# Ten 16 KB load slots become five of 32 KB, and the activation rows move to every eighth column

## The chip, the cores and the metric

The kernel runs on one core of a Trainium2 chip. The metric is the device time of one execution in microseconds (us), the median of several runs of the same program. Five engines of the core work side by side: TensorE (PE in the profile; its weight loads are PEld), VectorE (DVE), ScalarE (ACT), GpSimd (POOL) and SyncE (SP). Sixteen DMA engines carry data between device memory (DRAM) and the on-chip memory of 128 partitions. A DMA is issued by an engine's queue: SP issues all loads of weights and caches, ACT issues the load of `x`, and both issue the result. A DMA is cut into packets, here one for each contiguous run of a partition. In the trace a transfer of weights has 128 packets and sixteen landings, one for each engine's share; the instructions that read its data start after the last of the sixteen.

## What is computed

One decoding step of a transformer block for a batch of 4, one token each, in bf16:

```python
h  = x + attention(layernorm(x)) @ wo        # x: 4 x 1 x 1024
h2 = h + (silu(n @ w1) * (n @ w3)) @ w2      # n = layernorm(h)

# attention: 32 query heads of 128, 4 key/value heads, the last 2048 cached positions
q = layernorm(x) @ wq                        # wq: 1024 x 4096
p = softmax(q @ k.T * 128**-0.5)             # k, v: 4 x 4 x 2048 x 128 of the cache
o = p @ v                                    # wo: 4096 x 1024
# w1, w3: 1024 x 3584, w2: 3584 x 1024
```

The inputs that must be read are 55.57 MB: the two caches' windows, `wq` and `wo` 8.39 MB each (33.55 MB together), `w1`, `w3` and `w2` 7.34 MB each. Every byte is used once, with four rows of activations, so the arithmetic is small beside the reading.

## The kernel before

**The ring of loads.** The list `ring` names every load in its order: the keys of the four batch rows (`k`), the four parts of `wq` with four places `kT` for the transposed keys between them, the values `v`, `wo`, `w1`, `w3` and `w2`. `fill()` (line 118 of the profile issues the DMA) takes the next item while fewer than ten are open, gives it a slot of 8192 bf16 columns (16 KB on each partition, `NSLOT = 10`, `SLOT = 8192`), and issues its DMA from SP. `done(name, i)` marks an item as read and calls `fill()` again. A DMA waits on SP until the slot that it is given is free; as SP's queue is in order, all later loads wait behind it. A place `kT` has no DMA, but takes a slot. So there are 20 MB of slots, and the loads run some way ahead of the work.

The transfers are: `k`, `wq`, `v`, `wo` four each, of 2 MB in packets of 16 KB; `w1` and `w3` four each, of 1.75 MB in packets of 14 KB (two rows of 3584 columns a partition); `w2` five, of 8, 8, 8, 2 and 2 rows of 1024 columns (16 KB and 4 KB a partition). That is 29.

**The order of the work** is the order of the program text (the schedule is manual):

- `x` is loaded in four DMAs from ACT (line 134), a quarter of its columns each, to the partitions 32c to 32c+3. `layernorm_T` works on its transpose, where the batch is 4 of 32 columns.
- Keys: 256 transposes on PE (line 226), copied out of PSUM by DVE and ACT (lines 228, 230).
- `q`: for each part of `wq`, matmuls of 32 columns of activations against 512 columns of the weights, four of them side by side in the array (line 244). The four parts have 16 matmuls each.
- For each batch row scores (line 279), row maximum, softmax on ACT (line 319), transpose of the probabilities on DVE (line 331), output (line 354); the rows are staggered, so that the output of row b follows the scores of row b+3.
- `wo` (line 419), the sum with `x`, the second `layernorm_T`.
- `up_projection` for `w1`, then for `w3` (line 443), with silu on ACT and DVE in between (lines 457 to 461); the product `hg` (line 465) and its transpose `hg_T` (line 210, a helper).
- `w2` (line 476), the last sum `res` (line 486), and the result in four DMAs of four rows of 256 columns, two on SP and two on ACT (line 489).

Of the kernel before, what the change touches and what calls it, by code (L numbers as in the profile page):

```python
# [10 lines left out]
P = 128  # L11
ACT = mybir.ActivationFunctionType
ALU = mybir.AluOpType
AX = mybir.AxisListType
BF16 = mybir.dt.bfloat16
FP32 = mybir.dt.float32

NSLOT = 10
SLOT = 8192
NEG = -1.0e30  # L20


# [1 line left out]
def kernel(  # L24
# [20 lines left out]
    nc = tc.nc  # L45

    B, _, D = A_x.shape
    Hkv, Sk, Dh = A_k_cache.shape[1], A_k_cache.shape[2], A_k_cache.shape[3]
    NQ = A_wq.shape[1]
# [6 lines left out]
    NK = W // P  # L56
    C = 4
    R = 32
    DQ = D // C
    FQ = F // C  # L60
    FH = FQ // 2
# [8 lines left out]
    T = REP  # L70
# [18 lines left out]
    def of_cache(cache, b):  # L89
        return cache[b, :, Sk - W : Sk, :].rearrange("g (i j) d -> i g (j d)", j=JR)  # L90

    ks = [("k", b, [JR, Dh], of_cache(A_k_cache, b)) for b in range(B)]
    vs = [("v", b, [JR, Dh], of_cache(A_v_cache, b)) for b in range(B)]
    kts = [("kT", b, [JR, P], None) for b in range(B)]
    wqs = [("wq", i, [2, NQ], wq_v[:, 2 * i : 2 * i + 2, :]) for i in range(KC // 2)]
    wos = [("wo", g, [1, T * D], wo_v[:, g : g + 1, :]) for g in range(Hkv)]
    ring = ks + [x for two in zip(kts, wqs) for x in two] + vs + wos
    for name, w_v in (("w1", w1_v), ("w3", w3_v)):
        for i in range(KC // 2):
            ring.append((name, i, [2, F], w_v[:, 2 * i : 2 * i + 2, :]))  # L100
    W2B = [8, 8, 8, 2, 2]
    f0 = 0
    for i, n in enumerate(W2B):
        ring.append(("w2", i, [n, D], w2_v[:, f0 : f0 + n, :]))
        f0 += n
    place = {(name, i): at for at, (name, i, _, _) in enumerate(ring)}
    views = []
    used = set()

    def fill():  # L110

        while len(views) < len(ring) and (len(views) < NSLOT or len(views) - NSLOT in used):
            name, i, shape, src = ring[len(views)]
            slot = stream.tile([P, SLOT], BF16, tag="slot", name="s_" + name)
            dst = slot[:, : int(np.prod(shape))]
            view = dst.rearrange("p (a b) -> p a b", a=shape[0])
            if src is not None:
                nc.sync.dma_start(out=dst if name in ("k", "v") else view, in_=src)  # L118
            views.append(view)

    def get(name, i):
        return views[place[(name, i)]]

    def done(name, i):
        used.add(place[(name, i)])
        fill()

    ctx.enter_context(tc.manual_schedule())
# [1 line left out]

    x_nat = act.tile([P, DQ], BF16)
    nc.vector.memset(x_nat[:], 0.0)
    for c in range(C):
        nc.scalar.dma_start(out=x_nat[R * c : R * c + B, :], in_=x_flat[:, c * DQ : (c + 1) * DQ])
    fill()

    ident = const.tile([P, P], BF16)
# [39 lines left out]
    def layernorm_T(h_T, tag):  # L177

        both = act.tile([P, 2, KC, B], FP32, tag=tag + "_both")
        nc.vector.tensor_copy(out=both[:, 0], in_=h_T[:, :, :B])  # L180
        nc.vector.tensor_tensor(out=both[:, 1], in0=both[:, 0], in1=both[:, 0], op=ALU.mult)  # L181
        sums_ps = ps.tile([P, 2, KC, B], FP32, tag="kt3")
        nc.tensor.matmul(sums_ps[:], lhsT=ones_f[:], rhs=both[:], start=True, stop=True)  # L183
        sums = act.tile([P, 2, B], FP32, tag=tag + "_sums")
        nc.vector.tensor_reduce(
            out=sums[:], in_=sums_ps[:].rearrange("p t k b -> p t b k"), axis=AX.X, op=ALU.add
        )
        mean = act.tile([P, 2, B], FP32, tag=tag + "_mean")
        nc.vector.tensor_single_scalar(out=mean[:], in_=sums[:], scalar=1.0 / D, op=ALU.mult)
        rstd = act.tile([P, 1, B], FP32, tag=tag + "_rstd")  # L190
        nc.vector.tensor_tensor(out=rstd[:, 0], in0=mean[:, 0], in1=mean[:, 0], op=ALU.mult)
        nc.vector.tensor_tensor(out=rstd[:, 0], in0=mean[:, 1], in1=rstd[:, 0], op=ALU.subtract)  # L192
        nc.scalar.activation(  # L193
            out=rstd[:, 0], in_=rstd[:, 0], func=ACT.Sqrt, bias=eps_t[:], scale=1.0
        )
        nc.vector.reciprocal(out=rstd[:, 0], in_=rstd[:, 0])
        n_T = act.tile([P, KC, R], BF16, tag=tag + "_nT")
        nc.gpsimd.memset(n_T[:], 0.0)
        hc = act.tile([P, KC, B], FP32, tag=tag + "_hc")
        nc.vector.tensor_tensor(  # L200
            out=hc[:], in0=both[:, 0], in1=mean[:, 0:1, :].to_broadcast([P, KC, B]), op=ALU.subtract
        )
        nc.vector.tensor_tensor(
            out=n_T[:, :, :B], in0=hc[:], in1=rstd[:].to_broadcast([P, KC, B]), op=ALU.mult
        )
        return n_T

# [26 lines left out]

    q_ps = [ps.tile([P, REP // 2, Dh], FP32, tag=f"sc{hf}", name=f"q_ps{hf}") for hf in range(2)]
    HALF = REP // 2
    for i in range(KC // 2):
        w = get("wq", i)
        for kk in range(2):
            kc = 2 * i + kk  # L240
            for hf in range(2):
                for c in range(C):
                    o = (2 * c + hf) * HALF * Dh
                    nc.tensor.matmul(  # L244
                        q_ps[hf][R * c : R * c + R],
                        lhsT=xn_T[:, kc, :],
                        rhs=w[:, kk, o : o + HALF * Dh],
                        start=(kc == 0),
                        stop=(kc == KC - 1),
                        tile_position=(0, R * c),  # L250
                    )
        done("wq", i)
# [10 lines left out]
    for b in range(B):  # L263
        nc.vector.tensor_copy(  # L264
            out=Qm[:, b].rearrange("p (g y) -> p g y", y=QW)[:, :, :REP],
            in_=qT_ps[:, :, :, b].rearrange("p r g -> p g r"),
        )


# [122 lines left out]
    for l in range(2):  # L392
# [12 lines left out]
    oP = act.tile([P, Hkv, T, R], BF16)  # L405
    nc.gpsimd.memset(oP[:], 0.0)
    nc.vector.tensor_copy(
        out=oP[:, :, :, :B],
        in_=oX[:, :, : Hkv * B].rearrange("p t (g b) -> p g t b", b=B),
    )  # L410

# [21 lines left out]


    def up_projection(name, out_ps):
        for i in range(KC // 2):
            w = get(name, i)
            for kk in range(2):
                kc = 2 * i + kk
                for hf in range(2):  # L440
                    for c in range(C):
                        o = c * FQ + hf * FH
                        nc.tensor.matmul(  # L443
                            out_ps[hf][R * c : R * c + R],
                            lhsT=hn_T[:, kc, :],
                            rhs=w[:, kk, o : o + FH],
                            start=(kc == 0),
                            stop=(kc == KC - 1),
                            tile_position=(0, R * c),
                        )  # L450
            done(name, i)
# [32 lines left out]
            fc += 1  # L484
    res = act.tile([P, DQ], BF16)
    nc.vector.tensor_tensor(out=res[:], in0=y2_ps[:], in1=h1[:], op=ALU.add)  # L486
    for c in range(C):
        eng = nc.sync if c % 2 == 0 else nc.scalar
        eng.dma_start(out=out_flat[:, c * DQ : (c + 1) * DQ], in_=res[R * c : R * c + B, :])


# [28 lines left out]
```

## Time and profile before

| | before |
|---|---|
| median of three runs | 140.28 us (140.24 to 140.34) |
| the profiled execution | 140.35 us, of which the span shown is 138.5 us |
| packets of the SP and ACT queues' DMA, share of 16 engines | 94.8% of the span |
| read from DRAM | 55.58 MB, 401 GB/s over the span |
| PE busy, granted clock | 76.9 us (55%), 0.787 |
| DVE, ACT busy | 52.5 us, 43.2 us |
| transfers of weights and caches | 29 |

The span runs from the first to the last instruction. The 1.85 us between it and the profiled execution's time lie around it. The row of packets says how much of the sixteen DMA engines' time was taken by data. Busy times of the engines are sums over stages with different limits, so they are read beside the chain of work that ended last, which the profile follows back from the last instruction. For a transfer, the time from issue to landing holds its wait behind earlier transfers of the queue.

### The profile page before, as it was taken

How to read it: one execution, taken by the hardware profiler on the slowest of the kernel's cores; microseconds unless marked ns; L12 is line 12 of the kernel's file. 1: busy time of each engine (PE TensorE's matmuls, PEld its weight loads, DVE VectorE, ACT ScalarE, POOL GpSimd, SP SyncE). 2: the span in 40 equal slices, each digit the busy share in tenths (PEclk: the TensorE clock that was granted, in tenths of full speed). 3: DMA queues.
4: the chain of work that ended last, by engine and by line, in shares of the span. 5: the costliest groups of instructions: out<-in, count | busy, mean ns of one | idle time of the engine just before them, and what ended most of it. 6: DMA issues, size and time to landing. Idle time of an engine off the chain costs nothing.

```text
span 138.5 us, 2042 instructions
## 1 busy us (share of the span) xinstructions
PE 76.9 (55%) x868; PEld 45.8 (33%) x868; DVE 52.5 (38%) x97; ACT 43.2 (31%) x57; POOL 4.2 (3%) x18
## 2 busy tenths in 40 slices
PE   0009999971153799059639979483632432352280
PEld 0009988851011332024223535372311110142150
DVE  3026566630000334457365595515249700610001
ACT  2103799970000508999419600000420000000000
POOL 7400000000000000000000000000000000000000
PEclk9999999999555559955995999999999555555555
DMA  4999999999999999999999999999999999999940
GB/s 147 403 432 445 426 416 440 421 421 435 426 421 440 421 428 426 416 435 435 416 435 433 416 440 410 435 414 435 418 431 426 426 427 431 421 435 431 390 182 2
DMA packets 4249, 55.72 MB, mean 402 GB/s; under 512 B 496, under 2 KB 528, under 8 KB 784
## 3 DMA queue, kind: packets, MB, share of 16 engines
q1 hardware_dynamic: 4192, 55.58, 94.8%
q8 instruction: 7, 0.11, 0.3%
q10 hardware_dynamic: 48, 0.01, 0.0%
q14 instruction: 2, 0.02, 0.0%
HBM read 55.58 MB, written 0.01 MB: 401 GB/s over the span
## 4 chain that ended last, share of the span: by engine, by line
DMA 68%; PE 18%; DVE 6%; ACT 4%; issue 1%; SPq 1%; DVEq 0%
DMA s_w<-in_B_w_dram 38%; DMA s_wq<-in_A_wq_dram 24%; PE o_ps L354 10%; DMA s_k<-in_A_k_cache_dram 6%; ACT P L319 4%; PE sc_ps L279 4%; DVE PT L331 2%; PE q_ps L244 1%; PE nm_ps L308 1%; SPq L118 1%; DVE rmax L293 1%; PE mx_ps L295 1%; PE qT_ps L258 1%; DVE om L371 1%; PE tot_ps L340 1%
## 5 line engine op out<-in xcount | busy, mean ns | idle before, releaser
L319 ACT ACTIVATE P<-sc_ps,bias 128x512 bf16<-128x512 f32 x16 | 19.7, 1420 | 9.9 <-DVE bias L316 9.9
L226 PE MATMUL kt_ps<-ident,s_k 128*128 128x128 bf16 x256 | 18.4, 232 | 0.3
L226 PEld LDWEIGHTS <-s_k 128*128 128x128 bf16 x256 | 16.8, 105 | 1.9 <-issue 1.2
L354 PE MATMUL o_ps<-s_v,PT 128*128 128x512 bf16 x64 | 17.5, 435 | 0.0
L230 ACT COPY s_kT<-kt_ps 128x1024 bf16<-128x1024 bf16 x16 | 16.2, 1012 | 2.2 <-PE kt_ps L226 1.3
L443 PE MATMUL gu_ps<-s_w,n_T 128*32 128x448 bf16 x128 | 9.2, 435 | 13.4 <-DMA s_w<-in_B_w_dram 11.6
L228 DVE COPY s_kT<-kt_ps 128x1024 bf16<-128x1024 bf16 x16 | 11.1, 691 | 6.0 <-PE kt_ps L226 6.0
L476 PE MATMUL y_ps<-s_w,hg_T 128*32 128x256 bf16 x112 | 6.7, 416 | 9.4 <-DMA s_w<-in_B_w_dram 9.4
L244 PE MATMUL q_ps<-s_wq,n_T 128*32 128x512 bf16 x64 | 5.9, 503 | 10.4 <-DMA s_wq<-in_A_wq_dram 10.4
L331 DVE STREAM_TRANSPOSE PT<-P 128x2048 bf16<-128x2048 bf16 x4 | 9.2, 2302 | 2.7 <-ACT P L319 2.7
L354 PEld LDWEIGHTS <-PT 128*128 128x128 bf16 x64 | 7.1, 116 | 8.9 <-issue 4.2
L443 PEld LDWEIGHTS <-n_T 128*32 128x32 bf16 x128 | 3.9, 109 | 18.0 <-issue 14.6
L279 PE MATMUL sc_ps<-s_kT,Qm 128*32 128x512 bf16 x64 | 8.8, 608 | 0.4 <-DVE Qm L264 0.4
L193 ACT ACTIVATE rstd<-rstd,eps_t 128x4 f32<-128x4 f32 x2 | 0.6, 298 | 26.7 <-DVE rstd L192 26.7
L476 PEld LDWEIGHTS <-hg_T 128*32 128x32 bf16 x112 | 4.7, 138 | 11.7 <-issue 7.6
L183 PE MATMUL sums_ps<-both,ones_f 128*128 128x64 f32 x4 | 1.1, 374 | 11.9 <-DVE both L181 11.9
L254 DVE CAST q_sb<-q_ps 128x512 bf16<-128x512 f32 x1 | 0.7, 692 | 15.5 <-PE q_ps L244 15.5
L244 PEld LDWEIGHTS <-n_T 128*32 128x32 bf16 x64 | 2.0, 112 | 13.4 <-issue 12.7
L363 DVE SCALAR_TENSOR_TENSOR od<-o_ps,rinv,jmask 128x512 f32<-128x512 f32 x4 | 3.0, 750 | 8.0 <-PE o_ps L354 7.9
L295 PE MATMUL mx_ps<-ident_f,rmax 128*1 128x128 f32 x8 | 1.9, 333 | 7.4 <-DVE rmax L293 7.4
L459 DVE RECIPROCAL eg<-eg 128x896 f32<-128x896 f32 x1 | 5.8, 5754 | 0.0
L486 DVE TENSOR_TENSOR res<-y_ps,h 128x256 bf16<-128x256 f32 x1 | 0.4, 425 | 13.6 <-PE y_ps L476 13.6
(68 smaller groups left out, 62.4 us busy)
## 6 DMA issues: line engine op xcount, KB each, us to landing
s_w<-in_B_w_dram SPq DMA_DIRECT2D x8, 1792.0 KB, 25.4
s_k<-in_A_k_cache_dram SPq DMA_DIRECT2D x4, 2048.0 KB, 14.0
s_wq<-in_A_wq_dram SPq DMA_DIRECT2D x4, 2048.0 KB, 20.5
s_v<-in_A_v_cache_dram SPq DMA_DIRECT2D x4, 2048.0 KB, 27.9
s_wo<-in_A_wo_dram SPq DMA_DIRECT2D x4, 2048.0 KB, 27.4
s_w<-in_B_w_dram SPq DMA_DIRECT2D x3, 2048.0 KB, 32.7
s_w<-in_B_w_dram SPq DMA_DIRECT2D x2, 512.0 KB, 31.6
x_nat<-in_A_x_dram ACTq DMA_DIRECT2D x4, 2.0 KB
```

The lines of the kernel that those rows point to most:

```text
L226: nc.tensor.transpose(out=kt_ps[:, jj], in_=k[:, jb * JB + jj, :], identity=ident[:])
L228: nc.vector.tensor_copy(out=kT[:, jb * JB : (jb + 1) * JB], in_=kt_ps[:])
L230: nc.scalar.copy(out=kT[:, jb * JB : (jb + 1) * JB], in_=kt_ps[:])
L244: nc.tensor.matmul(q_ps[hf][R * c : R * c + R], lhsT=xn_T[:, kc, :], rhs=w[:, kk, o : o + HALF * Dh], start=(kc == 0), stop=(kc == KC - 1) ...
L279: nc.tensor.matmul(sc_ps[b][R * q : R * q + R], lhsT=Qm[:, b, g * R : (g + 1) * R], rhs=v[:, g, q], start=(g == 0), stop=(g == Hkv - 1), t ...
L295: nc.tensor.matmul(mx_ps[:1, :], lhsT=rmax[:], rhs=ident_f[:], start=True, stop=True)
L319: nc.scalar.activation(out=P4[:, :, :, g], in_=sc_ps[b][:].rearrange("p (j i) -> p j i", i=L5), func=ACT.Exp, bias=bias[:, g : g + 1], sca ...
L331: nc.vector.transpose(out=PT[:].rearrange("p j h -> p (j h)"), in_=stage.pop(("P4", b))[:].rearrange("p j i g -> p (j i g)"),)
L354: nc.tensor.matmul(o_ps[:], lhsT=PT[:, i * JM : (i + 1) * JM, :].rearrange("p j h -> p (j h)"), rhs=v[:, i * JM : (i + 1) * JM, :], start= ...
L443: nc.tensor.matmul(out_ps[hf][R * c : R * c + R], lhsT=hn_T[:, kc, :], rhs=w[:, kk, o : o + FH], start=(kc == 0), stop=(kc == KC - 1), til ...
L459: nc.vector.reciprocal(out=eg[:], in_=eg[:])
L476: nc.tensor.matmul(y2_ps[R * c : R * c + R, :], lhsT=hg_T[:, fc, :], rhs=w[:, ff, c * DQ : (c + 1) * DQ], start=(fc == 0), stop=(fc == FC ...
```

## The change

Five slots of 16384 columns (32 KB on each partition) take the place of ten of 8192, so the slots hold the same 20 MB. An entry of the ring is now a list of parts that share a slot: two of `k`, of `kT`, of `v` or of `wo`, each still with a DMA of its own of 2 MB; or one transfer of twice the rows: `wq` in two transfers of four rows (32 KB packets), `w1` and `w3` in two each (28 KB packets), `w2` in 16, 8, 2 and 2 rows, of which the last three share a slot. A slot is free when all of its parts have been read. The loops over `wq`, `w1` and `w3` run over two parts with four rows each, in place of four with two; the matmuls are the same in the same order.

`x` comes in one DMA of 16 rows of 256 columns, to every eighth partition (batch row b of column quarter c at partition 32c+8b, not 32c+b), so that in the transposed forms the batch lies at every eighth of 32 columns; the copies that read or write those columns use a stride of 8. The result goes out in two DMAs of eight rows, one on SP and one on ACT.

```diff
--- before.py
+++ after.py
@@ -15,8 +15,8 @@
 BF16 = mybir.dt.bfloat16
 FP32 = mybir.dt.float32
 
-NSLOT = 10
-SLOT = 8192
+NSLOT = 5
+SLOT = 16384
 NEG = -1.0e30
 
 
@@ -56,6 +56,7 @@
     NK = W // P
     C = 4
     R = 32
+    S = R // B
     DQ = D // C
     FQ = F // C
     FH = FQ // 2
@@ -89,40 +90,55 @@
     def of_cache(cache, b):
         return cache[b, :, Sk - W : Sk, :].rearrange("g (i j) d -> i g (j d)", j=JR)
 
-    ks = [("k", b, [JR, Dh], of_cache(A_k_cache, b)) for b in range(B)]
-    vs = [("v", b, [JR, Dh], of_cache(A_v_cache, b)) for b in range(B)]
-    kts = [("kT", b, [JR, P], None) for b in range(B)]
-    wqs = [("wq", i, [2, NQ], wq_v[:, 2 * i : 2 * i + 2, :]) for i in range(KC // 2)]
-    wos = [("wo", g, [1, T * D], wo_v[:, g : g + 1, :]) for g in range(Hkv)]
-    ring = ks + [x for two in zip(kts, wqs) for x in two] + vs + wos
-    for name, w_v in (("w1", w1_v), ("w3", w3_v)):
-        for i in range(KC // 2):
-            ring.append((name, i, [2, F], w_v[:, 2 * i : 2 * i + 2, :]))
-    W2B = [8, 8, 8, 2, 2]
+    def pair(parts):
+        return [parts[0:2], parts[2:4]]
+
+    k_, v_ = (
+        pair([(name, b, [JR, Dh], of_cache(cache, b)) for b in range(B)])
+        for name, cache in (("k", A_k_cache), ("v", A_v_cache))
+    )
+    kT_ = pair([("kT", b, [JR, P], None) for b in range(B)])
+    wo_ = pair([("wo", g, [1, T * D], wo_v[:, g : g + 1, :]) for g in range(Hkv)])
+
+    def four_rows(name, view, n):
+        return [[(name, i, [4, n], view[:, 4 * i : 4 * i + 4, :])] for i in range(KC // 4)]
+
+    wq_ = four_rows("wq", wq_v, NQ)
+    ring = k_ + wq_[:1] + kT_ + wq_[1:] + v_ + wo_ + four_rows("w1", w1_v, F) + four_rows("w3", w3_v, F)
+    W2B = [16, 8, 2, 2]
+    w2_ = []
     f0 = 0
     for i, n in enumerate(W2B):
-        ring.append(("w2", i, [n, D], w2_v[:, f0 : f0 + n, :]))
+        w2_.append(("w2", i, [n, D], w2_v[:, f0 : f0 + n, :]))
         f0 += n
-    place = {(name, i): at for at, (name, i, _, _) in enumerate(ring)}
-    views = []
+    ring += [w2_[:1], w2_[1:]]
+    views = {}
+    taken = []
     used = set()
 
     def fill():
 
-        while len(views) < len(ring) and (len(views) < NSLOT or len(views) - NSLOT in used):
-            name, i, shape, src = ring[len(views)]
-            slot = stream.tile([P, SLOT], BF16, tag="slot", name="s_" + name)
-            dst = slot[:, : int(np.prod(shape))]
-            view = dst.rearrange("p (a b) -> p a b", a=shape[0])
-            if src is not None:
-                nc.sync.dma_start(out=dst if name in ("k", "v") else view, in_=src)
-            views.append(view)
+        while len(taken) < len(ring):
+            n = len(taken) - NSLOT
+            if n >= 0 and not all((name, i) in used for name, i, _, _ in ring[n]):
+                break
+            parts = ring[len(taken)]
+            slot = stream.tile([P, SLOT], BF16, tag="slot", name="s_" + parts[0][0])
+            o = 0
+            for name, i, shape, src in parts:
+                dst = slot[:, o : o + int(np.prod(shape))]
+                o += int(np.prod(shape))
+                view = dst.rearrange("p (a b) -> p a b", a=shape[0])
+                if src is not None:
+                    nc.sync.dma_start(out=dst if name in ("k", "v") else view, in_=src)
+                views[(name, i)] = view
+            taken.append(slot)
 
     def get(name, i):
-        return views[place[(name, i)]]
+        return views[(name, i)]
 
     def done(name, i):
-        used.add(place[(name, i)])
+        used.add((name, i))
         fill()
 
     ctx.enter_context(tc.manual_schedule())
@@ -130,8 +146,7 @@
 
     x_nat = act.tile([P, DQ], BF16)
     nc.vector.memset(x_nat[:], 0.0)
-    for c in range(C):
-        nc.scalar.dma_start(out=x_nat[R * c : R * c + B, :], in_=x_flat[:, c * DQ : (c + 1) * DQ])
+    nc.scalar.dma_start(out=x_nat[::S, :], in_=x_flat.rearrange("b (c n) -> c b n", c=C))
     fill()
 
     ident = const.tile([P, P], BF16)
@@ -177,7 +192,7 @@
     def layernorm_T(h_T, tag):
 
         both = act.tile([P, 2, KC, B], FP32, tag=tag + "_both")
-        nc.vector.tensor_copy(out=both[:, 0], in_=h_T[:, :, :B])
+        nc.vector.tensor_copy(out=both[:, 0], in_=h_T[:, :, ::S])
         nc.vector.tensor_tensor(out=both[:, 1], in0=both[:, 0], in1=both[:, 0], op=ALU.mult)
         sums_ps = ps.tile([P, 2, KC, B], FP32, tag="kt3")
         nc.tensor.matmul(sums_ps[:], lhsT=ones_f[:], rhs=both[:], start=True, stop=True)
@@ -201,7 +216,7 @@
             out=hc[:], in0=both[:, 0], in1=mean[:, 0:1, :].to_broadcast([P, KC, B]), op=ALU.subtract
         )
         nc.vector.tensor_tensor(
-            out=n_T[:, :, :B], in0=hc[:], in1=rstd[:].to_broadcast([P, KC, B]), op=ALU.mult
+            out=n_T[:, :, ::S], in0=hc[:], in1=rstd[:].to_broadcast([P, KC, B]), op=ALU.mult
         )
         return n_T
 
@@ -234,10 +249,10 @@
 
     q_ps = [ps.tile([P, REP // 2, Dh], FP32, tag=f"sc{hf}", name=f"q_ps{hf}") for hf in range(2)]
     HALF = REP // 2
-    for i in range(KC // 2):
+    for i in range(KC // 4):
         w = get("wq", i)
-        for kk in range(2):
-            kc = 2 * i + kk
+        for kk in range(4):
+            kc = 4 * i + kk
             for hf in range(2):
                 for c in range(C):
                     o = (2 * c + hf) * HALF * Dh
@@ -263,7 +278,7 @@
     for b in range(B):
         nc.vector.tensor_copy(
             out=Qm[:, b].rearrange("p (g y) -> p g y", y=QW)[:, :, :REP],
-            in_=qT_ps[:, :, :, b].rearrange("p r g -> p g r"),
+            in_=qT_ps[:, :, :, S * b].rearrange("p r g -> p g r"),
         )
 
 
@@ -405,7 +420,7 @@
     oP = act.tile([P, Hkv, T, R], BF16)
     nc.gpsimd.memset(oP[:], 0.0)
     nc.vector.tensor_copy(
-        out=oP[:, :, :, :B],
+        out=oP[:, :, :, ::S],
         in_=oX[:, :, : Hkv * B].rearrange("p t (g b) -> p g t b", b=B),
     )
 
@@ -433,10 +448,10 @@
 
 
     def up_projection(name, out_ps):
-        for i in range(KC // 2):
+        for i in range(KC // 4):
             w = get(name, i)
-            for kk in range(2):
-                kc = 2 * i + kk
+            for kk in range(4):
+                kc = 4 * i + kk
                 for hf in range(2):
                     for c in range(C):
                         o = c * FQ + hf * FH
@@ -484,9 +499,9 @@
             fc += 1
     res = act.tile([P, DQ], BF16)
     nc.vector.tensor_tensor(out=res[:], in0=y2_ps[:], in1=h1[:], op=ALU.add)
-    for c in range(C):
-        eng = nc.sync if c % 2 == 0 else nc.scalar
-        eng.dma_start(out=out_flat[:, c * DQ : (c + 1) * DQ], in_=res[R * c : R * c + B, :])
+    out_v = out_flat.rearrange("b (c n) -> c b n", c=C)
+    nc.sync.dma_start(out=out_v[: C // 2], in_=res[: P // 2 : S, :])
+    nc.scalar.dma_start(out=out_v[C // 2 :], in_=res[P // 2 :: S, :])
 
 
 # ---- launch: one core; inputs and outputs as the reference has them ----
```

## The prediction, made before the changed kernel was run

> **What bounds the kernel now.** I read the page's slices first, then the chain that ended last, then the order of time around the places where PE waits for data, and last the waits of the queues.
>
> ```profile
> DMA  4999999999999999999999999999999999999940
> GB/s 147 403 432 445 426 416 440 421 421 435 426 421 440 421 428 426 416 435 435 416 435 433 416 440 410 435 414 435 418 431 426 426 427 431 421 435 431 390 182 2
> ...
> DMA 68%; PE 18%; DVE 6%; ACT 4%; issue 1%; SPq 1%; DVEq 0%
> ```
>
> The DMA engines are full from the second slice to the 38th, at 403 to 445 GB/s, with no hole at any stage. The chain names PE for 18% (the attention), yet the DMA row shows no gap there: the chain follows a wait for a free slot back into PE, while the queue still held work. So the end is set by when the last byte of `w2` lands, plus a tail. Evidence in order of time:
>
> ```profile
> 38.85 1.90 PE L244 MATMUL q_ps<-s_wq,n_T 128*32 128x512 bf16 x16 [3.85 <-DMA s_wq<-in_A_wq_dram]
> 43.75 1.90 PE L244 MATMUL q_ps<-s_wq,n_T 128*32 128x512 bf16 x16 [3.01 <-DMA s_wq<-in_A_wq_dram]
> ...
> 108.76 1.68 PE L443 MATMUL gu_ps<-s_w,n_T 128*32 128x448 bf16 x16 [3.36 <-DMA s_w<-in_B_w_dram]
> 113.06 1.69 PE L443 MATMUL gu_ps<-s_w,n_T 128*32 128x448 bf16 x16 [2.62 <-DMA s_w<-in_B_w_dram]
> ...
> 122.33 1.90 PE L476 MATMUL y_ps<-s_w,hg_T 128*32 128x256 bf16 x32 [3.22 <-DMA s_w<-in_B_w_dram]
> 127.22 1.90 PE L476 MATMUL y_ps<-s_w,hg_T 128*32 128x256 bf16 x32 [3.00 <-DMA s_w<-in_B_w_dram]
> 132.12 2.33 PE L476 MATMUL y_ps<-s_w,hg_T 128*32 128x256 bf16 x40 [3.00 <-DMA s_w<-in_B_w_dram]
> 134.61 0.62 PE L476 MATMUL y_ps<-s_w,hg_T 128*32 128x256 bf16 x8 [0.17 <-DMA s_w<-in_B_w_dram]
> 135.28 0.42 DVE L486 TENSOR_TENSOR res<-y_ps,h 128x256 bf16<-128x256 f32 x1 [13.61 <-PE y_ps L476]
> 135.73 0.66 SPq L489 DMA_DIRECT2D out_dram<-res  x2
> ```
>
> Wherever PE waits for DMA, its starts are one transfer apart: 4.90 us for 2 MB (38.85 to 43.75, 122.33 to 127.22), 4.30 us for 1.75 MB (108.76 to 113.06). Each stage is done 3 us before the next transfer lands. After the last landing come 0.66 us of matmuls, 0.45 us of `res`, then the result's DMAs and the end: 2.8 us from 135.73 to 138.5.
>
> **The change part by part.**
>
> *Seven transfers fewer.* `wq`, `w1` and `w3` lose two each, `w2` one: 29 become 22, with the same bytes. What does a transfer cost beside its bytes? I take it from the trace's landings, on engines that nothing disturbs: the first landings of neighbouring transfers are 4.886 to 4.902 us apart for 2 MB, 4.286 to 4.300 for 1.75 MB, 1.264 and 1.289 for the 0.5 MB parts of `w2`. The difference of the first two, 0.60 us for 16,384 bytes an engine (the 0.25 MB over sixteen), is 36.7 ps a byte. An engine's 131,072 bytes of a 2 MB transfer then take 4.81 us, which leaves 0.08; the 1.75 MB leave 0.08, the 0.5 MB 0.06 to 0.09. Last landings of the 0.5 MB parts are 1.23 apart and leave 0.03. So eight packets and the increment cost 0.03 to 0.09 us more than their bytes, whatever the packet's size from 4 to 16 KB. The packet records say the same from another side: medians of 160, 538 and 611 ns for 4, 14 and 16 KB lie on a line with some 10 ns at zero, and an increment takes 9 ns. If 28 and 32 KB packets stay on the line, each transfer saved is worth this fixed part: seven times 0.03 to 0.09 is 0.2 to 0.6; I take 0.06, from the middle, and get **−0.42 us** on the landing of the last byte. This lies on the path, since every engine is full to the end. No row shows a packet over 16 KB. A longer one could be slower: the nearest rows, 14 and 16 KB, differ by 0.1% in their rate a byte once the fixed part is off, which on the 64 us that the 27.3 MB concerned take (27.3 MB at 428 GB/s) is 0.06 us either way. An excess that no row suggests is kept as a rival.
>
> The Trainium skill, "DMA: Bandwidth & Descriptors", section "Why small descriptors are slow (HBM only)", speaks against as much gain: its fixed part is some 3 cycles a packet, and it finds merging worthwhile only at 256 bytes and below. With the 850 MHz that the same page gives the fabric, 3 cycles are 3.5 ns, and the 56 packets fewer on each engine an estimated 0.2 us, half of what I take from the landings. The landings decide, as they hold the increment and what lies between packets too.
>
> *Fewer, wider slots.* The danger is that SP waits for a slot until the queue has run dry. Slots are given out in the order in which they are first written, so `k`, `k`, the two `wq`, and the first `kT` pair take the five; the second `kT` pair takes the first keys' slot. Against the order of before, each load then waits as follows (its turn is the moment the data ahead of it has been carried, at 4.9 us a 2 MB). The first `v` pair: last key transposed, 29.2 against its turn at 43. Second `v` pair: first half of `q`, 38, turn 53. First `wo` pair: `q` done, 47.5, turn 62. Second `wo` pair: scores of row 1, 54, turn 72. First `w1`: scores of row 3, about 64, turn 82. Second `w1`: output of row 1, which ended at 77.84, plus 2, turn 90. First `w3`: output of row 3, 86.6 plus 2, turn 99. Second `w3` and the long `w2`: halves of `wo`, 95 and 97, turns 107 and 116. The rest of `w2`: the first half of `w1`, 102, turn 126. The 2 us are what the larger `wq` adds: after its last landing 32 matmuls are left in place of 16, at 1.90 us for 16. The smallest margin is 10 us. So no load comes late: 0.
>
> *Larger pieces for PE.* The last `w3` part leaves 32 matmuls behind its landing, in place of 16 at 1.68. `hg_T` was ready 4.3 us after the landing (117.43 to 121.73), now 6.0: 123.0 at a landing of 117.0. The long `w2` lands near 126.7; its 64 matmuls at 1.90 for 32 end at 130.5, and the 8-row part lands at 131.6. From there on the parts are those of before (8, 2, 2), so the tail is unchanged: 0. The cover is 1.1 us; past it, each 0.1 us late would be paid in full only if the later gaps (0.17 us before the last 8 matmuls) are used up too. The one gain possible: the granted clock is 0.5 over the last 32 us, and the burst of 3.8 us could raise it. Sixteen `q` matmuls took 1.05 us at full clock against 1.90, so the final 0.62 could become 0.35: −0.27 at best. In this trace a burst of 3.2 us (98.32 to 101.53) went at full clock because it began there; nothing shows that 3.8 us from cold suffices. I take 0.
>
> *`x` in one transfer.* The transpose of `x` waited until 9.12 us for it, and `sums_ps` and all key transposes stand behind that on PE. With four issues on ACT in place of one, three came after the first packets of the keys; one issue can land at 3 to 9 us, and PE starts at 8.6 rather than 10.5. Between 10 and 30 us PE is ahead of its next need anyway: 0 to the end. The packets are the same sixteen of 512 bytes (27 ns each); three increments of 9 ns fewer: 0. The strided copies on DVE (0.16 to 0.20 us a row for 32 to 128 columns) lie before 9.8 us and in the stage from 90 to 98.3, which the loads of `w1` and `w3` cover by 3 us at the next wait of PE; 0, at the price of 0.1 if that cover were gone.
>
> *The result in two transfers.* Before, each queue issued two, 0.34 and 0.27 us on SP. The first SP one had landed at 137.15, the second at 137.51: with nothing behind the first, −0.36 us. Against it: the issue has three dimensions now, and the nearest such rows, those of `v` with 128 rows, took 0.54 to 0.57 us against 0.33 for `wo`, so up to +0.24; and the rows may lie on fewer engines, all eight on one at worst, 0.22 us at 27 ns a packet. From −0.36 to +0.1; an issue of eight rows is nearer to the four of before than to 128, so **−0.2**.
>
> Here the skill's same page warns (section "Rules for kernel authors") that an outermost dimension of less than 16 confines a DMA to that many engines. The four-row DMAs had four landings of data each in the trace, in agreement. By the rule the eight rows of 2 by 4 would go over two engines with four packets each, and 27 ns a packet would add an estimated 0.1 us; the sum would be −0.1 in place of −0.2 for this part.
>
> **Sum.** −0.42 −0.2 = −0.62. The profiled execution took 140.35, a span of 138.5 and 1.85 around it, 0.07 above the median of 140.28. The span should become 137.9, that execution 139.7, and the median 139.66; I say 139.65.
>
> **Rivals.**
> (a) *The long packets save nothing*: they are carried as two, or the fixed part grows with length. For it: no row over 16 KB. Only the result's part is left, −0.36 to +0.1: 139.9 to 140.4, likeliest 140.1.
> (b) *The long packets are slower a byte*, slower than before. For it: last landings trail the first by 0.5 us at the first keys and by 1.7 at the end, so some engine is always held up, and a longer packet holds up longer what stands behind it. 64 us are concerned: 1% is +0.64 us and cancels the gain; 2% gives 140.9. Against it: the constant rate from 4 to 16 KB.
> (c) *A load waits for its slot and the DMA row shows a hole.* The largest shift I find is 2 us against a margin of 10; it would need the attention to run 8 us longer, say at half clock throughout, and each us beyond comes on top: 141.
> (d) *The gain is larger*: the tail's clock rises, 0.09 a transfer, −0.36 at the result: 0.6 + 0.36 + 0.27 = 1.2, 139.05.
>
> **How the numbers follow.** The forecast as summed holds 0.68, (d)'s upper parts 0.07, (a) 0.12, (b) 0.09, (c) 0.04. A measurement of this kernel tells about 0.2%, 0.28 us, from no change: 140.0 to 140.56 is the same. The forecast and (d) are faster, with 0.03 of (a): 0.78; the rest of (a) is the same, with 0.01 of (b): 0.10; the rest of (b), and (c), are slower: 0.12. The forecast's own range is 139.3 to 140.0 (−0.2 to −0.6 for the transfers, −0.36 to +0.1 for the result); the range given takes in (a) and the start of (b): 139.2 to 140.4.
>
> **What would show it.** The DMA row stays at 9 without a hole. On PE the start-to-start of neighbouring transfers of `w3` is 8.5 us, not twice 4.30; the last matmuls start near 134.2 in place of 134.61. From `res` to the end it takes 2.6 in place of 2.8 us. `x_T` starts well before 9 us, and changes nothing. It would be wrong if packets of 28 and 32 KB show more than 1.07 and 1.22 us (twice 538 and 611 ns), if PE's wait for the 8-row part of `w2` is gone, or if SP issues a load within a few us of its turn.

## The result: 0.3% faster, and the profile after

| | before | changed |
|---|---|---|
| median of 17 runs each, side by side | 140.42 us | 140.07 us |
| ratio, 95% interval | | 0.9971 (0.9964 to 0.9978) |
| profiled execution, its span | 140.35, 138.5 us | 140.13, 138.3 us |
| packets of weights and caches on each DMA engine | 232 | 176 |
| last part of `w2`: first of its sixteen landings | 132.85 us | 132.24 us |
| last part of `w2`: last of its sixteen landings | 134.57 us | 134.26 us |
| start of the result's DMAs to the end of the span | 2.80 us | 2.93 us |

The ratio is a gain of 0.41 us (0.31 to 0.51), where 0.62 was forecast; the medians alone differ by 0.35. (A median of 140.28 stood in front of the prediction; the 17 runs put it at 140.42.) The landings are read from the trace's records of each transfer's sixteen increments: an engine that has carried its share raises a semaphore with a packet of 4 bytes, 9 ns long in the trace.

The page of the changed kernel, DMA's slices and the chain that ended last:

```profile
DMA  4999999999989999999999999999999999999930
...
DMA 49%; PE 27%; DVE 13%; ACT 4%; SPq 3%; issue 2%; DVEq 0%
```

Of 37 full slices one reads 8 now, and the chain runs through more PE and DVE. That is no loss: as before, it follows waits for slots back into the attention, while the queue holds work. Around the slice that reads 8 the first landings keep their distance, 9.70 us for the 4 MB of `wq` and 4.90 for the next 2 MB. The row of the queue on the page of each kernel, before and changed (packets of every kind, MB, share of 16 engines):

```profile
q1 hardware_dynamic: 4192, 55.58, 94.8%
```

```profile
q1 hardware_dynamic: 3178, 55.58, 94.4%
```

The same bytes, a quarter fewer packets, a slightly smaller share of a shorter span. The end of the changed kernel in order of time:

```profile
117.17 3.18 PE L458 MATMUL gu_ps<-s_w,n_T 128*32 128x448 bf16 x32 [6.81 <-DMA s_w<-in_B_w_dram]
...
126.88 3.61 PE L491 MATMUL y_ps<-s_w,hg_T 128*32 128x256 bf16 x64 [6.53 <-DMA s_w<-in_B_w_dram]
...
131.77 2.33 PE L491 MATMUL y_ps<-s_w,hg_T 128*32 128x256 bf16 x40 [1.28 <-DMA s_w<-in_B_w_dram]
...
134.30 0.62 PE L491 MATMUL y_ps<-s_w,hg_T 128*32 128x256 bf16 x8 [0.20 <-DMA s_w<-in_B_w_dram]
...
134.97 0.42 DVE L501 TENSOR_TENSOR res<-y_ps,h 128x256 bf16<-128x256 f32 x1 [12.06 <-PE y_ps L491]
135.42 0.66 SPq L503 DMA_DIRECT2D out_dram<-res  x1
135.42 0.60 ACTq L504 DMA_DIRECT2D out_dram<-res  x1
```

Each PE line still ends its idle time on a DMA. The last matmuls start at 134.30 in place of 134.61: 0.31 us came from the loads. Then the new result, one DMA on each queue, takes 0.66 us to issue, as long as the two it replaces (0.34 and 0.27 on SP before), and from there to the end it is 0.13 us longer.

So two things had to be told apart: what in the ring of loads gains (slots, transfers or packets), and whether the result's part really costs.

### The profile page after: what moved, and what is told of

It is laid out like the page before. It is cut to its first block, busy times and chain, and to the rows that moved or that the text cites. A ratio compares the mean times of both kernels' runs of the same rounds, so it can differ in the third digit from the quotient of the medians.

```text
span 138.3 us, 2012 instructions
## 1 busy us (share of the span) xinstructions
PE 80.2 (58%) x866; PEld 47.5 (34%) x868; DVE 52.9 (38%) x97; ACT 42.7 (31%) x57; POOL 4.2 (3%) x18
## 4 chain that ended last, share of the span: by engine, by line
DMA 49%; PE 27%; DVE 13%; ACT 4%; SPq 3%; issue 2%; DVEq 0%
DMA s_wq<-in_A_wq_dram 29%; DMA s_w<-in_B_w_dram 20%; PE o_ps L369 10%; PE y_ps L434 5%; ACT P L334 4%; PE sc_ps L294 3%; DVE PT L346 3%; SPq L133 3%; PE gu_ps L458 2%; PE q_ps L259 2%; DVE om L386 2%; DVE od L378 2%; PE on_ps L409 1%; PE tot_ps L355 1%; PE nm_ps L323 1%
## 5 line engine op out<-in xcount | busy, mean ns | idle before, releaser
L241 PE MATMUL kt_ps<-ident,s_k 128*128 128x128 bf16 x256 | 17.3, 228 | 1.3 <-ACT s_kT L245 1.0
L241 PEld LDWEIGHTS <-s_k 128*128 128x128 bf16 x256 | 16.3, 103 | 2.3 <-issue 1.7
L245 ACT COPY s_kT<-kt_ps 128x1024 bf16<-128x1024 bf16 x16 | 15.7, 1012 | 2.5 <-PE kt_ps L241 2.5
L458 PE MATMUL gu_ps<-s_w,n_T 128*32 128x448 bf16 x128 | 10.7, 513 | 8.8 <-DMA s_w<-in_B_w_dram 6.8
L259 PE MATMUL q_ps<-s_wq,n_T 128*32 128x512 bf16 x64 | 7.0, 615 | 11.8 <-DMA s_wq<-in_A_wq_dram 11.8
L458 PEld LDWEIGHTS <-n_T 128*32 128x32 bf16 x128 | 4.7, 131 | 14.1 <-issue 11.6
L259 PEld LDWEIGHTS <-n_T 128*32 128x32 bf16 x64 | 2.7, 137 | 15.6 <-issue 15.5
L434 PE MATMUL y_ps<-s_wo,oP 128*32 128x256 bf16 x128 | 6.5, 397 | 1.7 <-DVE oP L422 1.7
L270 ACT CAST q_sb<-q_ps 128x512 bf16<-128x512 f32 x1 | 0.6, 585 | 17.8 <-PE q_ps L259 17.8
```

The lines of the kernel that those rows point to most:

```text
L241: nc.tensor.transpose(out=kt_ps[:, jj], in_=k[:, jb * JB + jj, :], identity=ident[:])
L245: nc.scalar.copy(out=kT[:, jb * JB : (jb + 1) * JB], in_=kt_ps[:])
L259: nc.tensor.matmul(q_ps[hf][R * c : R * c + R], lhsT=xn_T[:, kc, :], rhs=w[:, kk, o : o + HALF * Dh], start=(kc == 0), stop=(kc == KC - 1) ...
L434: nc.tensor.matmul(y_ps[R * c : R * c + R, :], lhsT=oP[:, g, t, :], rhs=w[:, 0, o : o + DQ], start=(g == 0 and t == 0), stop=(g == Hkv - 1 ...
L458: nc.tensor.matmul(out_ps[hf][R * c : R * c + R], lhsT=hn_T[:, kc, :], rhs=w[:, kk, o : o + FH], start=(kc == 0), stop=(kc == KC - 1), til ...
```

## Experiments

### The parts by themselves

*The result in four DMAs again*, all else as changed:

```diff
-    nc.sync.dma_start(out=out_v[: C // 2], in_=res[: P // 2 : S, :])
-    nc.scalar.dma_start(out=out_v[C // 2 :], in_=res[P // 2 :: S, :])
+    for c in range(C):
+        eng = nc.sync if c % 2 == 0 else nc.scalar
+        eng.dma_start(out=out_flat[:, c * DQ : (c + 1) * DQ], in_=res[R * c : R * c + R : S, :])
```

> The changed kernel with the result in four DMAs again, one for each column quarter, two on SP and two on ACT (rows still at every eighth column). Theory A (the pair of eight-row DMAs is a loss: in the two profiles the stretch from the start of the result's DMAs to the end of the span went from 2.80 to 2.93 us): the stretch is back at 2.80, and the kernel some 0.13 us faster than the changed one, ratio to before about 0.996. Rival B (the stretch differs by the chance of one profile, and the pair of DMAs costs or gains nothing): the ratio stays at 0.997 and the stretch at 2.9. Rival C (two DMAs are a gain, as the prediction had it): slower than the changed kernel by 0.2 us, ratio 0.9985.

Measured: 141.02 us, ratio 1.0031 (1.0021 to 1.0040). All three theories were wrong about this one: it is 0.8 us slower than the changed kernel. From the start of the result's DMAs to the end it takes 3.88 us, against 2.93. The reason shows in the rows of the tile `res`; first this kernel (durations of one issue in ns, least, median and largest), then the ring-only kernel below, which issues four DMAs of the same shape:

```profile
L504 SPq DMA_DIRECT2D out_dram<-res x2: 742/750/757, 135.3 to 136.1; - x2
L504 ACTq DMA_DIRECT2D out_dram<-res x2: 588/628/669, 135.3 to 136.0; - x2
```

```profile
L505 SPq DMA_DIRECT2D out_dram<-res x2: 274/310/347, 135.2 to 135.6; - x2
L505 ACTq DMA_DIRECT2D out_dram<-res x2: 282/288/295, 135.2 to 135.5; - x2
```

The same four rows of 512 bytes take 0.59 to 0.76 us to issue where the rows lie eight partitions apart, and 0.27 to 0.35 where they are neighbours. The first packet follows 1.31 us after the issue begins, against 0.76. So the price is the layout's, not the number of dimensions': these issues have two dimensions, and on SP four such rows cost 0.75 us, where eight rows in one DMA of three dimensions cost 0.66. With the rows at every eighth partition, two DMAs are right; with neighbouring rows, four cost no more.

*The ring alone.* The changed kernel with the rows of before:

```diff
-    nc.scalar.dma_start(out=x_nat[::S, :], in_=x_flat.rearrange("b (c n) -> c b n", c=C))
+    for c in range(C):
+        nc.scalar.dma_start(out=x_nat[R * c : R * c + B, :], in_=x_flat[:, c * DQ : (c + 1) * DQ])
...
-        nc.vector.tensor_copy(out=both[:, 0], in_=h_T[:, :, ::S])
+        nc.vector.tensor_copy(out=both[:, 0], in_=h_T[:, :, :B])
...
-    nc.sync.dma_start(out=out_v[: C // 2], in_=res[: P // 2 : S, :])
-    nc.scalar.dma_start(out=out_v[C // 2 :], in_=res[P // 2 :: S, :])
+    for c in range(C):
+        eng = nc.sync if c % 2 == 0 else nc.scalar
+        eng.dma_start(out=out_flat[:, c * DQ : (c + 1) * DQ], in_=res[R * c : R * c + B, :])
```

> The kernel before with only the ring changed: five slots of 32 KB and seven transfers fewer; x in four DMAs, the result in four, rows at neighbouring columns. Theory A: the whole gain sits here, -0.31 us by the last landing of w2 (134.57 to 134.26 in the two profiles) up to -0.6 us by the first one (132.85 to 132.24): ratio 0.9957 to 0.998, and at least as fast as the changed kernel. Rival: x in one transfer, which starts PE 0.7 us earlier, is needed for the gain: ratio near 1.000. The first landing of the last w2 transfer should be near 132.24 us in both kernels with the new ring.

Measured: 139.81 us, ratio 0.9949 (0.9937 to 0.9961). The whole gain sits in the ring, and it is larger than in the changed kernel, and a little larger than the 0.9957 to 0.998 that theory A gave. The last part of `w2` lands from 132.37 to 134.03 us.

*The rows alone*: the ring of before with the new rows, `x` in one DMA and the result in two (the reverse of the diff above).

> The kernel before with only the rows at every eighth column, x in one DMA and the result in two; ten slots of 16 KB and 29 transfers. Theory A: nothing on the loads (first landing of the last w2 transfer near 132.85), +0.13 us at the result: ratio 1.001. The prediction's view: -0.2 us, ratio 0.9986. Rival: x in one DMA gains at the head, ratio below 0.999 with the stretch of the result at 2.9.

Measured: 140.51 us, ratio 1.0000 (0.9992 to 1.0009); landings 132.81 to 134.66. Neither loss nor gain, and the −0.2 us of the prediction's view lies outside the interval. From the start of the result's DMAs to their last landing it takes 1.98 us, against 1.78 before; from there to the end 0.84 against 1.02. In the trace SP ends with five waits for pairs of semaphores, one after the other, and here the awaited semaphore stands in the last pair, before in the second. In the changed kernel it stands in the third: 1.99 and 0.94. So the result's part costs 0.13 us there and 0.02 here. `x_T` starts at 8.36 us in place of 9.12, and nothing comes of it.

### Slots, transfers or packets

*Each big transfer as two*, in the slots of the changed kernel:

```diff
-                if src is not None:
+                if name[0] == "w" and name != "wo" and shape[0] in (4, 16):
+                    h = shape[0] // 2
+                    for e in range(2):
+                        nc.sync.dma_start(out=view[:, e * h : e * h + h], in_=src[:, e * h : e * h + h])
+                elif src is not None:
```

> The changed kernel with each of the seven big transfers issued as two (29 transfers and packets of 14 and 16 KB as before, in the five slots of 32 KB). Theory A (a transfer and its packets cost 0.06 to 0.09 us beside their bytes, and that is the whole gain): first landing of the last w2 transfer back at 132.85, ratio 1.001 (the result's 0.13 us is left). Rival (the slots, or the earlier issue of the loads, make the gain): landing stays near 132.24, ratio 0.997.

Measured: 140.41 us, ratio 0.9997 (0.9988 to 1.0005). Landings 132.96 to 134.66; its first packet started 0.2 us later than the others', at 2.37. The gain is gone, so it is not the slots'.

*Transfers of double size, packets of the old size.* The ring-only kernel, where the two halves of a partition's row are put a little apart in the slot, so that one DMA has two packets a partition:

```diff
-SLOT = 16384
+PAD = 32
+SLOT = 16384 + 2 * PAD
...
+                if name[0] == "w" and name != "wo" and shape[0] in (4, 16):
+                    half = int(np.prod(shape)) // 2
+                    pad = 256 if name in ("w1", "w3") else PAD
+                    dst = slot[:, : 2 * (half + pad)].rearrange("p (e x) -> p e x", e=2)[:, :, :half]
+                    nc.sync.dma_start(out=dst, in_=src.rearrange("p (e a) b -> p e (a b)", e=2))
+                    views[(name, i)] = dst.rearrange("p e (a b) -> p e a b", a=shape[0] // 2)
+                    continue
...
```

The matmuls then read the two halves of a row; nothing else differs from the ring-only kernel.

> The ring-only kernel (five slots, 22 transfers, x and the result in four DMAs each, ratio 0.9949) with the halves of each of the seven big transfers put 64 or 512 bytes apart in the slot, so that a transfer is one DMA still but has packets of 14 and 16 KB, as before. Theory P (the cost beside the bytes is one of each packet): the gain is gone, ratio 0.999 to 1.000, first landing of the last w2 transfer 132.8. Theory T (the cost is one of each transfer): the gain stays, ratio 0.995, landing 132.3. By packet records alone, 10 ns at zero length, 56 packets on an engine would be 0.56 us; an increment of 9 ns for seven transfers 0.06.

Measured: 140.40 us, ratio 0.9998 (0.9989 to 1.0006); first landing 132.76. Theory P: with 22 transfers, but the packets of before, nothing is left of the gain. The queue's row is that of before but for the increments of seven transfers:

```profile
q1 hardware_dynamic: 4080, 55.58, 94.8%
```

*The step in the other direction*: the kernel before with the parts of `wq`, `w1`, `w3` and the 8-row parts of `w2` issued as two DMAs each (an edit like the halves above), then with one DMA of two packets a partition (an edit like the padding above, with 16 columns of padding in `wq` and `w2`).

> The kernel before with each part of wq, w1, w3 and the three 8-row parts of w2 issued as two DMAs: 44 transfers in place of 29, their packets 7 and 8 KB. The same step as the change, in the other direction and 15 merges in size: 15 times 0.06 to 0.09 us, +0.9 to +1.3 us, ratio 1.006 to 1.010, first landing of the last w2 transfer 133.7 to 134.2. A rival in which the old packets lie on a flat part of the curve, and only the wider slots or fewer waits of SP matter: ratio 1.000 to 1.002.

> The kernel before with its 29 transfers, but the two halves of each part of wq, w1, w3 and the 8-row parts of w2 put 32 or 512 bytes apart in the slot: packets of 7 and 8 KB, 120 more on an engine. Theory P: as with 44 transfers, less 15 increments of 9 ns: +0.8 to +1.2 us, ratio 1.006 to 1.009. Theory T: ratio 1.000.

Measured: 141.69 us, ratio 1.0095 (1.0081 to 1.0108), and 141.51 us, ratio 1.0082 (1.0069 to 1.0096). Both as theory P has it; 15 transfers more add little to their packets. The rows of the queue, halves first:

```profile
q1 hardware_dynamic: 6352, 55.58, 95.1%
```

```profile
q1 hardware_dynamic: 6112, 55.58, 95.1%
```

All kernels in one table, by the first landing of the last part of `w2`, which the engines that come late do not delay. Executions also begin their loads at slightly different times (the keys' second transfer first lands at 12.55 to 12.86 us), so the last column counts from that landing:

| packets of loads on an engine | transfers | first landing, us | after the keys' second transfer, us |
|---|---|---|---|
| 176 | 22 | 132.24 to 132.37 (five profiles: changed twice, result in four, ring only twice) | 119.53 to 119.58 |
| 184 | 23 | 132.14 (ring with the short end, below) | 119.59 |
| 232 | 22 | 132.76 (ring, padded) | 120.10 |
| 232 | 29 | 132.81, 132.85, 132.96 (rows only, before, halves) | 120.02, 120.08, 120.10 |
| 352 | 29 | 133.83 (before, padded) | 121.07 |
| 352 | 44 | 133.99 (before, halves) | 121.19 |

By the last column, where the mean of the first row is 119.55 and that of the 232 packets in 29 transfers 120.07: at 22 transfers, 56 packets more cost 0.55 us, 9.8 ns each; at 29 transfers, 120 packets more cost 1.00 us, 8.4 ns each. At 352 packets, 15 transfers more cost 0.12 us, 8 ns each; an increment's record is 9 ns. The packet records agree: two packets of half the length take 9 to 11 ns more than one, at each step that the traces hold (medians 160, 311 and 612 ns for 4, 8 and 16 KB, 274, 538 and 1065 ns for 7, 14 and 28 KB, 1214 ns for 32 KB). So a packet costs 8 to 10 ns beside its bytes from 4 to 32 KB, and a transfer little more than its own increment (at 232 packets, seven transfers more show no cost at all).

### Again, and a version that beats both

*The changed kernel and the ring-only kernel once more.*

> The changed kernel once more beside the kernel before. If the difference between it (ratio 0.9971) and the ring-only kernel (0.9949) is real, 0.9971 comes again, with the result's DMAs taking 0.66 us to issue and 2.8 to 2.95 us from their start to the end of the span; if it was the chance of one chip, near 0.995.

> The ring-only kernel once more. In single profiles the last w2 transfer's landings spread over 1.66 us here (first to last engine) and over 2.02 and 1.96 us in the changed kernel. If that spread belongs to the rows and to x in one DMA, it is 1.6 to 1.7 again and the ratio 0.995; if it is the chance of an execution, it lies anywhere from 1.6 to 2.0, and the ratio near 0.996.

Measured: the changed kernel 139.95 us, ratio 0.9971 (0.9961 to 0.9980); ring-only 139.59 us, ratio 0.9939 (0.9926 to 0.9953), each beside its own runs of the kernel before. The difference of 0.2 to 0.3% is real: the intervals don't meet in either pair. Part of it is the result: 2.94 us from the start of its DMAs to the end in the changed kernel, 2.76 in ring-only. The spread of the last landings was 1.96 and 1.62 us, as in the first profiles. But the rows alone had 1.85, and ring-only kernels with other packets 1.93 (padded) and 1.90 (below), all with their share of the chance of an execution; so whether the rows make the spread wider stays open.

These profiles also show a thing that one profile hides. The changed kernel, first profile in stages (start and end, length, busy time of PE, PEld, DVE, ACT and POOL with their counts, then granted clock, DMA share, GB/s), then its second:

```profile
126.00:131.00 5.00, 3.61 (x64) 2.88 (x64) 0.00 (x0) 0.00 (x0) 0.00 (x0) 0.50 0.97 410
131.00:138.30 7.30, 2.94 (x48) 1.90 (x47) 0.42 (x1) 0.00 (x0) 0.00 (x0) 0.50 0.24 95
```

```profile
126.00:131.00 5.00, 3.30 (x64) 2.67 (x64) 0.00 (x0) 0.00 (x0) 0.00 (x0) 0.62 0.97 410
131.00:138.10 7.10, 1.86 (x48) 1.18 (x47) 0.42 (x1) 0.00 (x0) 0.00 (x0) 0.90 0.25 98
```

and the last matmuls of the second:

```profile
134.32 0.40 PE L491 MATMUL y_ps<-s_w,hg_T 128*32 128x256 bf16 x8 [0.84 <-DMA s_w<-in_B_w_dram]
```

In the second, the clock rose at 129.79, within the burst of 64 matmuls for the long part of `w2`, and the last eight matmuls took 0.40 us in place of 0.62. In both, the clock's records change at steps of 3.41 us. These steps, two of the first profile and two of the second, in the same columns:

```profile
125.42:128.84 3.42, 1.96 (x40) 1.71 (x43) 0.00 (x0) 0.00 (x0) 0.00 (x0) 0.50 1.01 431
128.84:132.25 3.41, 2.12 (x44) 1.59 (x40) 0.00 (x0) 0.00 (x0) 0.00 (x0) 0.50 0.83 341
```

```profile
61.53:64.94 3.41, 2.85 (x16) 1.55 (x10) 2.12 (x4) 2.96 (x7) 0.00 (x0) 0.50 1.04 442
126.38:129.79 3.41, 2.86 (x56) 2.41 (x59) 0.00 (x0) 0.00 (x0) 0.00 (x0) 0.50 0.94 399
```

In the first profile the burst was split over two steps, with 1.96 and 1.65 us of it, and the clock stayed at half; in the second it filled 2.86 us of the step that ended at 129.79. So the same kernel can run 0.22 us faster or slower by where the burst falls. The Trainium skill, "TensorE: Matmul & The Clock Gate", section "Part 1: The HAM clock gate (the "warmup" mystery)", describes a free-running window of 3413 ns that must be busy; the steps in the records have that length. At this place seven profiles hold the burst in one piece: the clock rose in the five where one step held 2.86 us of it or more, and not in the two where none held over 2.13 us of matmuls. But how busy a step must be does not come out of these traces: the step at 61.53, with 2.85 us of matmuls in other shapes, did not raise the clock.

*A shorter end.* The ring-only kernel with the last rows of `w2` cut once more:

```diff
-    W2B = [16, 8, 2, 2]
+    W2B = [16, 8, 2, 1, 1]
```

> The ring-only kernel with w2 in 16, 8, 2, 1 and 1 rows: the last landing has 4 matmuls behind it in place of 8 (0.62 us at half clock for 8), for one transfer and 8 packets on an engine more (0.08 us). If both terms hold: 0.1 to 0.25 us faster than ring-only, ratio 0.9935 to 0.9945. If the last landing's own fixed latency is the bound, as fast as ring-only or 0.08 us slower.

Measured: 139.48 us, ratio 0.9926 (0.9914 to 0.9938), beside 0.9939 for ring-only in the same comparison. The two intervals overlap, so a gain by the cut itself, 0.11 us between the medians, is not shown; but the kernel is clearly faster than the one before and the changed one. Its last four matmuls, then the last eight of the ring-only kernel beside it:

```profile
134.09 0.29 PE L492 MATMUL y_ps<-s_w,hg_T 128*32 128x256 bf16 x4 [0.35 <-DMA s_w<-in_B_w_dram]
```

```profile
134.01 0.40 PE L492 MATMUL y_ps<-s_w,hg_T 128*32 128x256 bf16 x8 [0.82 <-DMA s_w<-in_B_w_dram]
```

They took 0.29 us against 0.40, both with the clock raised.

## Why the prediction was right, point by point

**The bound** was right. In every kernel the last matmuls wait for the last landing, and 120 packets more moved it by 1.1 and 1.2 us with the PE's work unchanged.

**"Seven transfers fewer", −0.42 us.** The sign and the mechanism were right, the size too small for undisturbed engines: 0.52 us by the table. The step had divided the fixed part by transfers and taken 0.06 from a span of 0.03 to 0.09, where the lower end came from the last landings of the small parts; the larger transfers had said 0.08. The unit was the packet, 8 to 10 ns each, 56 of them; the prediction left open whether it was the packets or the transfers. At the last landing the changed kernel kept only 0.31 and 0.29 us, as its slowest engine trailed by 2.0 us in place of 1.7; the ring-only kernels kept 0.54 and 0.60. The rule of the Trainium skill that was weighed in the prediction ("DMA: Bandwidth & Descriptors", section "Why small descriptors are slow (HBM only)") gave an estimated 3.5 ns a packet; the runs show 8 to 10, and show that longer runs still pay at 14 to 32 KB where every engine is full to the end. The page's limit of 256 bytes is for joining consecutive pieces into one packet; here the pieces themselves grew, so the runs don't test it as it stands.

**Rivals (a) and (b)**, long packets that save nothing or go slower, fell: medians of 1065 and 1214 ns for 28 and 32 KB against 1076 and 1222 for two small ones. Nor do the long packets make the slowest engine's lag, which was (b)'s ground: in both profiles of the changed kernel it stood at 1.82 and 1.74 us at the keys' last transfer, before a packet over 16 KB had landed.

**"Fewer, wider slots", 0.** Right. Rival (c) didn't come: the three later parts of `w1` and `w3` and the long part of `w2` landed at least 20.9 us after their issue, of which their own carrying takes 8.5 to 9.7; so each was issued 12 us or more ahead of its turn. The shift of PE was larger than the 2 us worked out: the second layer norm's result came at 102.82 in place of 98.32, in part as the matmuls of `wo` fell into a time of half clock, up to 98.12 us. Before, in order of time, and changed, in the chain that ended last:

```profile
90.73 3.68 PE L419 MATMUL y_ps<-s_wo,oP 128*32 128x256 bf16 x128 [1.48 <-DVE oP L407]
```

```profile
92.28 6.54 PE y_ps L434 x104
```

The margin, 10 us by the prediction and 12 as measured, bore it.

**"Larger pieces for PE", 0.** Right in the profile that went with the result: `hg_T` was ready at 122.96 (123.0 was forecast), the 64 matmuls ended at 130.5, the 8-row part came at 131.77. But the gain that was set at 0, "nothing shows that 3.8 us from cold suffices", comes in some executions: −0.22 us in the second profile. What suffices, and when, is open (see above).

**"`x` in one transfer", 0.** Right for the end. The transpose of `x` started at 8.37, not long before the 9.12 of before, and PE began on the keys at 9.8, not at 8.6: the packets of `x` came at 5.6 to 7.8 us, among the keys' all the same.

**"The result in two transfers", −0.2 us.** This step failed: +0.13 us in the changed kernel, +0.02 with the rows alone. It counted one issue less, and held eight rows to be nearer to the four of before than to the 128 of `v`. One issue of eight rows eight partitions apart takes 0.66 us, as long as the two issues before, and the first packets come 1.24 us after it begins, against 0.76. So nothing was saved at the issue, and the data set out later. The skill's rule in the prediction (same page, section "Rules for kernel authors") was right here: 8 packets and 2 increments of each result DMA are in the trace, so two engines, by the rule with four packets each.

**The sum.** The packets' 0.52 us less the result's 0.13 is 0.39, and the ratio shows 0.41. The forecast was 0.62: its first term was too small by 0.10 and its second wrong in sign, off by 0.33. That the two errors cancel in part is luck. Nor does the time by itself tell the forecast from rival (a): 140.07 is what (a) gave (likeliest 140.1), and lies outside the forecast's own 139.3 to 140.0, because the runs of the kernel before had a median of 140.42 and not 140.28; it is the landings and the packet medians that decide for the forecast. And the agreement of 0.39 with 0.41 is kinder than it looks: in a single execution the clock of the tail (0.22 us) and the lag of the slowest engine (0.3 us) come on top, and the two profiles' spans are 0.18 and 0.37 us shorter than the one before. The ring-only kernel gained more than its packets, 0.72 and 0.86 us, with a lag of 1.66 and 1.62 us and, in the second profile, the clock raised. What decides the lag is not settled.

## What to carry to other kernels

Where all DMA engines are full to the end, count packets, not transfers: each cost 8 to 10 ns beside its bytes at any length from 4 to 32 KB here, on every engine, and longer contiguous runs for each partition were a small gain in every pair that was run. Look at what else such a change needs: here the layout of the small rows wasn't needed for it, and cost what it was to save, since a DMA of a few rows spaced eight partitions apart took twice the time to issue. A last landing is that of the slowest engine; compare first and last landings before a gain or its lack is put down to the change.

## What was not expected

- The price of partition spacing at the issue: 0.59 to 0.76 us for four or eight rows at every eighth partition, 0.27 to 0.35 us for four neighbouring ones, on both queues.
- Sixteen engines with the same bytes end 1.6 to 2.0 us apart. In the trace a 16 KB packet of instructions (queue q8, the first at 20.4 to 21.6 us) takes one engine's time, about 1 us; in the profile before, the spread of a transfer's landings goes from 0.51 to 1.56 us at the keys' last transfer, which it falls into, and stays. In all twelve profiles no engine is over 0.7 us late before that packet, one is after it, and the number grows with the later ones to seven or eight at the end. That these packets make the lag was not tested by an experiment, and what sets its size (1.6 to 2.0 us) is open.
- Where a burst of 3.3 to 3.6 us falls on steps of 3.41 us decides whether the clock rises in the last 8 us. It is worth 0.22 us where the clock is still up at the last matmuls; in two profiles (result in four, ring padded) it rose and was back at half before them, and the last eight took 0.62 us.
